# Another order of operations from the third batch on, in a linear-attention and leaky-ReLU MLP kernel on one Trainium2 core

## The chip, the cores and the metric

The kernel runs on one core of one Trainium2 chip. A core has five engines with a row of instructions each: TensorE (PE in the profile) for matrix products, VectorE (DVE), ScalarE (ACT), GpSimd (POOL), and SyncE (SP), which here only starts transfers (DMAs). The metric is the device time of one execution in microseconds (us). Before the change the median of 3 runs is 271.83 us, the lowest 271.36 and the highest 273.06.

## What is computed

A linear attention with cosine weights over 8 batch elements, 8 heads, 576 tokens and 64 channels, and a two-layer MLP (512 to 2048 to 512, leaky ReLU) on its result, 4608 tokens in all. All inputs and the output are 32-bit floats; the reference, cut to what matters:

```python
def phi(x, c, s):                       # c, s: cos and sin of pi/2 * position / 576
    r = np.maximum(x, 0.0)
    return np.concatenate([r * c, r * s], axis=-1)
q_p, k_p = phi(q, cos_w, sin_w), phi(k, cos_w, sin_w)
kv = np.einsum('bhsf,bhsd->bhfd', k_p, v)
z = np.sum(k_p, axis=2)
num = np.einsum('bhsf,bhfd->bhsd', q_p, kv)
den = np.einsum('bhsf,bhf->bhs', q_p, z)[..., None] + 1e-06
x = (num / den).transpose(0, 2, 1, 3).reshape(B * S, H * D)
h = x @ w_in
g = np.maximum(0.01 * h, h)
return g @ w_out
```

## The kernel before

**Groups of tokens.** The tokens are worked on in nine groups, g = 0 to 8. Groups 0 to 7 ("batch g") are the first 512 tokens of each batch element, in four parts j of 128; group 8 gathers the last 64 tokens of all eight elements. Each group goes through the same stages:

- q and k are loaded (`load(q,g)`, L280; `load(k,g)` and `load(v,g)`, L294). `q_prep(g,j,0,8,E)` (L418 on DVE or POOL, L416 on ACT) makes the two halves of phi(q), by the cosine and by the sine, for part j on engine E: D is DVE, A is ACT, P is POOL. `k_cos(b,j,E)` and `k_sin(b,j,E)` (the same lines) make one half of phi(k) each, for one of nine token columns j, and `v_pairs(b,lo,hi,E)` (L424 on ACT, L426 on the others) converts head pairs lo to hi of v to 16 bits, beside a column of ones that yields z.
- `kv_sum(b,0,4)` (L493) is phi(k)^T v: 72 small matmuls, two pairs of heads after the other two.
- phi(q) is transposed by DMA, two parts at a time: `q_transpose_dma(g,0)` for parts 0 and 1 and `q_transpose_dma(g,1)` for parts 2 and 3 (L530, qpT<-qp).
- `num(g,j)` (L577) multiplies the transposed phi(q) with kv, 8 matmuls; `den`, `rec` and `mul` (L587, L593, L601, all DVE) divide, which gives xs.
- `x_transpose_dma(g)` (L544, xT<-xs) transposes all four parts of x at once by DMA; batch 2 does it on PE with `x_transpose`.
- The first MLP layer is done by Strassen's scheme with seven products in place of eight, `P(g,u,n)` (L781): n is the product, 1 to 7, and u = 0 to 3 a quarter of the 2048 columns; each is 4 matmuls of 256 columns. `x_sum(g,n,E)` makes the sums of x that the scheme needs, and `w1_sum`, `weight_sum` those of the weights (all L674).
- `e(g,u,x)` brings the products out of PSUM, the memory that PE writes: b and s are copies (lower case on ACT, L424; capital on DVE, L426), w and y are additions on DVE (L674), and a, c, e and d are leaky ReLUs on ACT (L813) that write G.
- The second layer is done in the same way: `g_sum` makes sums of G (DVE), `F(g,i)` (L900) is half of a product, four matmuls, `R(g,n,E)` turns a finished product into a result (DVE additions L674; ACT copies L424), and `S(g,n)` (L964) stores a quarter of the group's output.

Groups 0 and 1 are done with other code (`M`, `h`, `f2` and others), which the change leaves alone, but F and R of batch 1 run beside batch 2 and 3 and are touched by the order.

**What sets the order.** Each operation is an entry in a long text, `PROGRAM` (L25 to L154), which is parsed and carried out entry by entry; the compiler may not reorder (`manual_schedule`). So every engine gets its instructions in the order of the entries, and works through them in that order: an instruction that waits holds up all behind it on its engine. Between engines there are only semaphores for the data and the buffers.

```python
    for name, args in parse(PROGRAM):
        OPS[name](*args)
```

All loads, stores and DMA transpositions of the part in question sit in one row on SyncE. The pools bound how far ahead it can be (the number is that of buffers):

```python
    stage = pool("stage", 4)
    kppool = pool("kpp", 1)
    qppool = pool("qpp", 2)
    qptpool = pool("qpT", 2)
    xspool = pool("xs", 1)
    xtpool = pool("xT", 2)
    opool = pool("osb", 4)
    ps_o = pool("ps_o", 2, PS)
    ps_n = pool("ps_n", 1, PS)
```

`stage` holds what the loads bring of q, k and v, and a load waits for the oldest of its four buffers. In PSUM, `ps_n` holds the two halves of one num or kv_sum, `ps_o` the sums of the second layer, and four more banks belong to P. These four open with batch 2's first product and use the memory that batch 1 had until then (`early`, closed in `banks`, L750), among it the sum that R(1,7) reads.

Of the kernel before, what the change touches and what calls it, by code (L numbers as in the profile page):

```python
# [55 lines left out]
g_sum(1,3,0,6) den(2,1) rec(2,1) k_sin(3,3,D) mul(2,1) R(1,6,D) k_cos(3,8,D) k_cos(3,5,P) k_sin(3,7,P) k_cos(3,0,P)
F(1,16) F(1,14) v_pairs(3,0,2,A) k_cos(3,3,A) q_prep(3,3,0,8,A) x_transpose(2,0,A) F(1,17) den(2,2) k_cos(3,2,D)
num(2,3) x_transpose(2,1,A) rec(2,2) mul(2,2) F(1,18) F(1,15) x_transpose(2,2,A) q_transpose_dma(3,0) load(q,4)
F(1,19) k_sin(3,2,D) k_cos(3,6,D) k_sin(3,6,A) k_cos(3,7,D) den(2,3) rec(2,3) v_pairs(3,2,4,D) mul(2,3) F(1,7)
# [1 line left out]
num(3,0) F(1,20) den(3,0) x_sum(2,2,P) rec(3,0) e(2,0,s) mul(3,0) P(2,0,6) P(2,0,2) F(1,21) P(2,1,1) x_sum(2,3,P)
q_transpose_dma(3,1) e(2,0,a) e(2,0,w) P(2,0,3) e(2,0,e) g_sum(1,4,0,8) num(3,1) x_sum(2,4,D) P(2,0,7) load(k,4)
P(2,1,5) F(1,22) e(2,1,b) den(3,1) rec(3,1) e(2,0,y) e(2,0,c) P(2,1,2) P(2,0,4) P(2,1,6) mul(3,1) e(2,1,S) e(2,1,a)
num(3,2) F(1,23) e(2,0,d) e(2,1,w) den(3,2) rec(3,2) mul(3,2) P(2,2,1) P(2,1,3) P(2,1,7) num(3,3) P(2,2,5) F(1,24)
R(1,4,D) den(3,3) q_prep(4,0,0,8,A) e(2,1,e) e(2,2,b) e(2,1,y) rec(3,3) P(2,2,6) mul(3,3) P(2,2,2) P(2,1,4) F(1,25)
e(2,2,s) e(2,1,c) e(2,1,d) e(2,2,w) e(2,2,a) P(2,2,3) w1_sum(1,3,D) P(2,3,1) q_prep(4,2,0,8,P) P(2,2,7) e(2,2,e)
P(2,3,5) load(v,4) q_prep(4,1,0,8,P) F(1,26) q_prep(4,3,0,8,D) e(2,2,y) g_sum(2,1,0,4,1) e(2,3,b) P(2,3,6) P(2,3,2)
F(1,27) e(2,3,s) k_cos(4,4,A) e(2,3,w) P(2,2,4) P(2,3,7) e(2,2,c) e(2,2,d) x_transpose_dma(3) P(2,3,3) F(2,0)
k_cos(4,7,D) g_sum(2,1,4,8,2) e(2,3,y) g_sum(2,2,4,8,2) e(2,3,a) x_sum(3,1,D) e(2,3,e) e(2,3,c) P(2,3,4) P(3,0,1)
k_cos(4,3,P) k_sin(4,3,P) x_sum(3,2,P) e(2,3,d) P(3,0,5) k_cos(4,1,A) k_sin(4,4,A) k_sin(4,1,A) e(3,0,s) R(1,3,D)  # L70
e(3,0,B) g_sum(2,1,5,8,2) g_sum(2,2,0,4,1) g_sum(2,2,5,8,2) F(2,1) P(3,1,1) F(2,2) P(3,0,6) P(3,0,2) F(2,3) F(2,4)
F(2,5) k_sin(4,8,A) k_cos(4,6,A) k_cos(4,8,A) e(3,0,a) R(2,1,A) e(3,0,w) x_sum(3,3,D) v_pairs(4,2,4,D) x_sum(3,4,D)
P(3,0,3) e(3,0,e) e(3,1,B) P(3,0,7) F(2,6) P(3,1,5) F(2,8) P(3,1,2) e(3,0,y) P(3,0,4) k_cos(4,0,A) k_sin(4,6,A)
k_sin(4,0,A) e(3,1,s) e(3,0,d) k_sin(4,2,P) k_cos(4,5,P) k_sin(4,5,D) v_pairs(4,0,2,D) F(2,7) P(3,1,6)
g_sum(2,3,0,4,1) e(3,1,w) R(2,6,D) e(3,0,c) e(3,1,a) k_cos(4,2,P) k_sin(4,7,P) load(q,5) q_transpose_dma(4,0)
# [5 lines left out]
P(3,2,7) x_transpose_dma(4) e(3,2,e) F(2,16) q_prep(5,0,0,8,P) q_prep(5,1,0,8,A) e(3,3,b) k_sin(5,1,D) R(2,7,D)
k_cos(5,4,D) e(3,2,y) e(3,3,s) q_transpose_dma(5,0) F(2,17) F(2,18) P(3,3,6) P(3,2,4) v_pairs(5,2,4,D) F(2,19)
load(k,6) e(3,3,w) e(3,2,c) q_prep(5,2,0,8,A) k_sin(5,8,A) g_sum(2,4,4,8) R(2,5,D) g_sum(2,4,0,4) k_sin(5,0,D) F(2,20)
P(3,3,7) F(2,21) P(3,3,2) e(3,2,d) q_prep(5,3,0,8,A) e(3,3,a) F(2,22) P(3,3,3) F(2,23) F(2,24) e(3,3,e) e(3,3,y)
F(2,25) P(4,0,1) k_sin(5,5,P) k_cos(5,7,P) e(4,0,b) x_sum(4,1,P) k_cos(5,0,P) F(2,26) P(3,3,4) P(4,0,5) F(2,27)
k_sin(5,3,D) v_pairs(5,0,2,D) R(2,4,D) q_transpose_dma(5,1) x_sum(4,3,D) x_sum(4,2,D) k_cos(5,2,A) e(3,3,c)
k_cos(5,3,D) R(2,3,D) e(3,3,d) e(4,0,s) F(3,0) P(4,0,6) P(4,0,2) F(3,1) e(4,0,w) g_sum(3,1,5,8,2) g_sum(3,1,0,4,1)
F(3,2) k_sin(5,4,A) k_cos(5,8,A) e(4,0,a) P(4,0,3) g_sum(3,3,5,8,2) g_sum(3,2,0,4,1) P(4,1,1) P(4,0,7) F(3,3) P(4,1,5)
q_prep(6,0,0,8,P) e(4,0,e) e(4,1,b) k_sin(5,2,A) x_sum(4,4,D) g_sum(3,2,5,8,2) R(3,1,A) e(4,0,y) g_sum(3,1,4,8,2)
g_sum(3,2,4,8,2) q_prep(6,1,0,8,A) e(4,1,S) F(3,4) kv_sum(5,0,4,n) e(4,0,c) P(4,1,6) P(4,1,2) F(3,5) P(4,0,4) e(4,1,w)  # L90
e(4,0,d) e(4,1,a) num(5,0) P(4,1,7) F(3,6) P(4,1,3) F(3,7) P(4,2,1) F(3,8) P(4,2,5) num(5,2) F(3,9) den(5,0) e(4,1,y)
P(4,1,4) rec(5,0) g_sum(3,3,4,8,2) k_cos(6,2,D) mul(5,0) g_sum(3,3,0,4,1) R(3,6,D) den(5,2) q_prep(6,2,0,8,A) e(4,1,c)
e(4,1,e) e(4,2,b) rec(5,2) P(4,2,6) F(3,10) mul(5,2) F(3,12) num(5,1) e(4,2,s) e(4,2,w) e(4,1,d) F(3,13) P(4,3,1)
F(3,11) P(4,2,2) P(4,2,3) num(5,3) F(3,14) den(5,1) k_cos(6,5,P) k_sin(6,6,A) k_cos(6,4,A) rec(5,1) g_sum(3,4,0,4)
mul(5,1) k_cos(6,0,D) k_sin(6,0,D) k_cos(6,7,P) k_sin(6,5,P) k_cos(6,3,P) den(5,3) k_sin(6,8,D) R(3,2,A) e(4,2,a)
k_cos(6,6,P) rec(5,3) k_cos(6,1,D) mul(5,3) F(3,16) P(4,3,5) P(4,2,7) e(4,2,e) S(2,4) load(v,6) S(2,5) S(2,3)
q_transpose_dma(6,0) S(2,2) x_transpose_dma(5) e(4,3,b) e(4,2,y) q_prep(6,3,0,8,A) e(4,3,S) load(q,7) P(4,3,6)
P(4,3,2) k_sin(6,1,P) k_sin(6,2,P) k_sin(6,4,D) e(4,3,w) F(3,17) F(3,15) P(4,2,4) F(3,18) S(3,2) P(4,3,3) k_sin(6,3,D)
F(3,19) e(4,3,a) k_cos(6,8,A) e(4,2,c) R(3,7,D) k_sin(6,7,D) g_sum(3,4,4,8) R(3,5,D) g_sum(4,1,4,8,2) F(3,20)
v_pairs(6,2,4,A) v_pairs(6,0,2,A) e(4,2,d) F(3,22) P(4,3,7) F(3,21) kv_sum(6,0,4,n) e(4,3,y) g_sum(4,1,0,4,1)  # L100
g_sum(4,2,0,4,1) x_sum(5,1,D) g_sum(4,2,4,8,2) x_sum(5,2,P) x_sum(5,3,P) F(3,23) P(4,3,4) R(3,4,D) e(4,3,c) e(4,3,e)
num(6,0) F(3,24) e(4,3,d) F(3,25) P(5,0,1) F(3,26) F(3,27) e(5,0,b) R(3,3,D) P(5,0,6) P(5,0,5) P(5,0,2) P(5,1,1)
F(4,0) e(5,0,S) g_sum(4,1,5,8,2) e(5,0,w) x_sum(5,4,D) den(6,0) rec(6,0) g_sum(4,2,5,8,2) e(5,0,a) F(4,1) F(4,2)
P(5,0,7) F(4,4) P(5,0,3) P(5,1,5) F(4,3) q_transpose_dma(6,1) F(4,5) num(6,1) e(5,0,e) R(4,1,A) mul(6,0) e(5,0,y)
e(5,1,B) den(6,1) q_prep(7,2,0,8,D) rec(6,1) mul(6,1) F(4,6) P(5,1,2) P(5,1,6) e(5,1,s) q_prep(7,0,0,8,A) F(4,8)
P(5,0,4) e(5,1,a) e(5,0,d) e(5,0,c) e(5,1,w) F(4,7) P(5,2,5) num(6,2) P(5,1,3) P(5,1,7) load(k,7) F(4,9)
g_sum(4,3,0,4,1) den(6,2) R(4,6,D) k_cos(7,8,D) rec(6,2) e(5,1,y) mul(6,2) e(5,2,S) e(5,1,e) F(4,10) F(4,11) P(5,2,1)
e(5,2,b) P(5,1,4) S(3,5) F(4,12) P(5,2,6) P(5,2,2) num(6,3) g_sum(4,3,5,8,2) R(4,2,A) e(5,1,d) e(5,2,a) e(5,1,c)
load(v,7) g_sum(4,3,4,8,2) e(5,2,w) q_prep(7,3,0,8,P) q_prep(7,1,0,8,P) F(4,13) k_sin(7,5,P) k_sin(7,1,P) k_cos(7,5,P)
den(6,3) k_sin(7,0,D) P(5,2,3) S(3,3) P(5,3,1) P(5,3,5) P(5,2,7) rec(6,3) mul(6,3) g_sum(4,4,0,4) e(5,2,e) e(5,2,y)  # L110
# [1094 lines left out]
```

## Time and profile before

| what | us |
|---|---|
| median of 3 runs | 271.83 |
| lowest, highest of them | 271.36, 273.06 |
| the profiled execution's own time | 273.01 |
| its span, first to last instruction | 271.2 |
| of the chain of work that ended last: PE, DMA | 86%, 9% |
| PE's granted clock, whole span | 1.00 |

The profile is that of one execution, which took 273.01 us in all; the times in its rows count from the start of its span of 271.2. The chain of work that ended last is found by going back from the last instruction to whatever released each one. Busy time is that of each engine, and a row of a group gives the line, the engine, the operation, the tile written and the tile read, the shape, and the number of instructions. The first 64 us or so of the span (groups 0 and 1, and kv_sum of batch 2) are the same in both kernels.

### The profile page before, as it was taken

To read this page: it belongs to the slowest core of one execution; us is meant where nothing else is said; L and a number is where in the kernel's file an instruction comes from. 1 tells how busy PE (TensorE), PEld (TensorE's weight loads), DVE (VectorE), ACT (ScalarE), POOL (GpSimd) and SP (SyncE) were. 2 spreads that over 40 slices of the span, in tenths; PEclk is the share of its full clock that TensorE was granted. 3 is DMA by queue.
4 is the path that set the end of the run, shared out by engine and by line. 5 is a ranking of instruction groups with operands and counts; after the bars stand their busy time and mean duration, and the time that the engine had idled before them with its cause. 6 is when DMAs were issued, how large, how long until landed. Compare 5 with 4: busy or idle time off the path is not lost.

```text
span 271.2 us, 7148 instructions
## 1 busy us (share of the span) xinstructions
PE 262.5 (97%) x2925; PEld 223.0 (82%) x2925; DVE 210.7 (78%) x446; ACT 174.0 (64%) x308; POOL 103.1 (38%) x87
## 2 busy tenths in 40 slices
...
GB/s 219 370 395 414 379 398 372 389 243 246 240 246 324 160 182 311 310 209 241 283 153 209 199 361 166 140 118 142 139 92 217 0 80 77 77 3 76 43 80 116
DMA packets 75040, 57.08 MB, mean 210 GB/s; under 512 B 47232, under 2 KB 63616, under 8 KB 74624
## 3 DMA queue, kind: packets, MB, share of 16 engines
...
q14 instruction: 9, 0.07, 0.1%
...
## 4 chain that ended last, share of the span: by engine, by line
PE 86%; DMA 9%; ACT 1%; DVE 1%; SPq 1%; issue 0%
PE ps L900 32%; PE ps_f L781 29%; PE ps_h L624 10%; PE ps_o L648 5%; DMA qpT<-qp 4%; DMA vst<-in_v_dram 3%; DMA xT<-xs 3%; PE ps_num L577 3%; PE ps_kv L493 2%; PE ps_f L900 1%; PE ps_xT L1054 1%; PE ps_kv L1005 1%; PE ps_numh L1040 1%; PE ps_qt L566 1%; PE ps_idle L358 0%; ACT vm L424 0%
## 5 line engine op out<-in xcount | busy, mean ns | idle before, releaser
L813 ACT ACTIVATE G<-ps_f 128x512 f16<-128x512 f32 x84 | 48.6, 597 | 31.0 <-PE ps_f L781 30.6
L900 PE MATMUL ps<-w,G 128*128 128x256 f16 x496 | 68.4, 273 | 0.0
L900 PEld LDWEIGHTS <-G 128*128 128x128 f16 x640 | 61.4, 98 | 6.2
L781 PEld LDWEIGHTS <-w 128*128 128x128 f16 x448 | 48.8, 114 | 2.2 <-DMA xT<-xs 0.7
L781 PE MATMUL ps_f<-xT,w 128*128 128x256 f16 x336 | 49.3, 273 | 1.0 <-DVE ext L674 0.5
L781 PEld LDWEIGHTS <-wsum 128*128 128x128 f16 x336 | 36.3, 114 | 0.7
L900 PE MATMUL ps<-T,ext 128*128 128x256 f16 x240 | 33.2, 273 | 0.0
L624 PE MATMUL ps_h<-xT,w 128*128 128x512 f16 (+1 forms) x144 | 29.1, 355 | 0.0
L900 PEld LDWEIGHTS <-ext 128*128 128x128 f16 x256 | 24.8, 98 | 2.6
L781 PE MATMUL ps_f<-X,wsum 128*128 128x256 f16 x176 | 26.2, 273 | 0.0
L674 DVE TENSOR_TENSOR ps_f<-ps_f,s 128x512 f32<-128x512 f32 x28 | 19.5, 695 | 8.1 <-PE ps_f L781 5.8
L624 PEld LDWEIGHTS <-w 128*128 128x128 f16 x144 | 15.9, 114 | 10.9
L418 POOL TENSOR_SCALAR kp<-kst,cos_t 128x256 f16<-128x256 f32 (+1 forms) x17 | 20.8, 1229 | 7.7 <-PE ps_f L781 3.0
L674 DVE TENSOR_TENSOR y<-ps_f,s 128x512 f32<-128x512 f32 x28 | 19.1, 682 | 5.0 <-PE ps_f L781 4.9
L418 POOL TENSOR_SCALAR kp<-kst,sin_t 128x256 f16<-128x256 f32 x15 | 18.5, 1239 | 5.9 <-DMA kst<-in_k_dram 5.9
L635 ACT ACTIVATE G<-ps_h 128x1024 f16<-128x1024 f32 x16 | 15.9, 1022 | 7.2 <-PE ps_h L624 7.2
L674 DVE TENSOR_TENSOR osb<-ps,ext 128x512 f32<-128x512 f32 x23 | 15.7, 685 | 5.0 <-PE ps L900 4.9
L601 DVE TENSOR_TENSOR xs<-ps_num,rden 128x512 f16<-128x512 f32 x28 | 19.2, 687 | 0.5
L813 ACT ACTIVATE G<-y 128x512 f16<-128x512 f32 x28 | 17.7, 631 | 3.0 <-DVE y L674 2.9
L424 ACT COPY ps_f<-ps_f 128x512 f32<-128x512 f32 x22 | 12.5, 570 | 8.6 <-PE ps_f L781 7.7
L900 PE MATMUL ps<-ext,G 128*128 128x256 f16 x128 | 17.7, 273 | 0.0
L424 ACT COPY s<-ps_f 128x512 f32<-128x512 f32 x21 | 12.4, 589 | 7.5 <-DVE y L674 4.1
(120 smaller groups left out, 451.3 us busy)
## 6 DMA issues: line engine op xcount, KB each, us to landing
...
qst<-in_q_dram SPq DMA_DIRECT2D x7, 1024.0 KB, 10.3
kst<-in_k_dram SPq DMA_DIRECT2D x5, 1152.0 KB, 7.3
vst<-in_v_dram SPq DMA_DIRECT2D x5, 1152.0 KB, 9.1
w2st<-in_moe_w_out_dram SPq DMA_DIRECT2D x3, 1024.0 KB, 13.9
...
```

What stands on the lines that cost most here:

```text
L418: eng.tensor_scalar(out=o, in0=i, scalar1=0.0, scalar2=col, op0=ALU.max, op1=ALU.mult)
L424: nc.scalar.copy(o, i)
L493: nc.tensor.matmul(ps[:, o, (c - lo) * NE : (c - lo + 1) * NE], lhsT=st["kp", b][sl, c, j, :], rhs=vm[sl, c, j, :], start=(j == 0), stop=( ...
L577: nc.tensor.matmul(ps[lo:hi, h // 4, (h % 4) * NE : (h % 4 + 1) * NE], lhsT=qpT[:, h, lo:hi], rhs=kv[b][:, h, :],)
L601: nc.vector.tensor_tensor(out=xs(), in0=ps[:, :, 0 : 4 * NE].rearrange("p a (b e) -> p a b e", e=NE)[:, :, :, 0:D], in1=st["rden", *k].rea ...
L624: nc.tensor.matmul(ps[:, m % 2, lo:hi], lhsT=w1[m // 4, c][0][:, w1[m // 4, c][1], m % 4 : 512 : 4], rhs=xT[:, lo // P : hi // P, c, :], s ...
L635: nc.scalar.activation(st["g", g][:, m - 1 : m + 1, :], ps, AF.Lrelu)
L648: nc.tensor.matmul(st["ps_o", g, tt], lhsT=st["g", g][:, m, tt * P : (tt + 1) * P], rhs=w2[:, m, :], start=(m == 0), stop=(m == NFT - 1),)
L674: eng.tensor_tensor(out=o, in0=a, in1=b, op=op)
L781: nc.tensor.matmul(ps[:, mi * HT : (mi + 1) * HT], lhsT=a[:, c, 2 * r0 + mi : 512 : 4], rhs=b[:, c], start=(n in (1, 5) and mi == 0 and c ...
L813: nc.scalar.activation(st["g", g][:, m : m + 2, r * HT : (r + 1) * HT], {"a": A, "c": y22, "e": E, "d": B_}[e].rearrange("p (m t) -> p m t ...
L900: nc.tensor.matmul(ps[:, tt], lhsT=a[:, i, tt * P : (tt + 1) * P], rhs=b[:, i], start=(first and i == 4 * halves[0]), stop=(i == NPR - 1 a ...
```

## The change

The entries of `PROGRAM` behind `num(2,0)` (L52) stand in another order, up to the end; the functions stay as they are. The entries are the same 1128, and PE's row has the same 5852 instructions, weight loads with them, in another order. 66 entries get another engine: 17 go from DVE to ACT, 12 from POOL to ACT, 11 from POOL to DVE, 10 from DVE to POOL, 8 from ACT to DVE and 8 from ACT to POOL. By kind they are 22 k_cos, 20 k_sin, 10 copies of e (6 from DVE to ACT, 4 back), 8 x_sum, 3 v_pairs and 3 q_prep. Three places of the diff, with the rest left out:

```diff
...
-k_cos(3,4,D) x_transpose(2,3,A) kv_sum(3,0,4,n) R(1,2,D) x_sum(2,1,D) R(1,7,D) R(1,5,D) P(2,0,1) e(2,0,b) P(2,0,5)
...
+x_transpose(2,3,A) kv_sum(3,0,4,n) R(1,7,D) x_sum(2,1,D) R(1,2,D) R(1,5,D) x_sum(2,2,D) P(2,0,1) e(2,0,b) load(q,4)
...
-load(k,5) S(1,4) S(1,5) q_transpose_dma(4,1) load(v,5) S(1,2) S(1,3) load(q,6) kv_sum(4,0,4,n) P(3,1,3) P(3,1,7)
...
+v_pairs(4,2,4,A) P(3,0,4) P(3,1,2) e(3,0,d) load(k,5) q_transpose_dma(4,0) load(q,5) e(3,1,w) F(2,7) R(2,6,D)
...
+k_cos(5,0,A) q_prep(5,1,0,8,A) k_cos(5,5,A) q_prep(5,2,0,8,A) e(3,2,c) x_transpose_dma(4) load(q,6) F(2,17) P(3,3,6)
...
```

**DVE at the start of batch 2's products.** The rows run from the last conversions for kv_sum(3) to the results of batch 1. vm<-vst is v_pairs(3,2,4); the first osb row is R(1,2), ext<-ps_7 is R(1,7), the second osb row R(1,5), and X1<-xT is x_sum(2,1). Before:

```order
L426 CAST vm_167<-vst_1079 128x18x64
L601 TENSOR_TENSOR xs_1194<-ps_num_1236,rden_1280 128x512
L418 TENSOR_SCALAR kp_1117<-G0_95,cos_t_159 128x4x64
L674 TENSOR_TENSOR osb_1368<-ps_7_1081,ext_93 128x512
L674 TENSOR_TENSOR X1_179<-xT_1227 128x512
L674 TENSOR_TENSOR ext_93<-ps_7_1111,ext_93 128x512
L674 TENSOR_TENSOR osb_1372<-ps_7_1167,ext_93 128x512
```

Now:

```order
L593 RECIPROCAL rden_1278<-den_1270 128x8
L601 TENSOR_TENSOR xs_1176<-ps_num_1233,rden_1278 128x512
L674 TENSOR_TENSOR ext_93<-ps_7_1111,ext_93 128x512
L674 TENSOR_TENSOR X1_179<-xT_1220 128x512
L674 TENSOR_TENSOR osb_1368<-ps_7_1081,ext_93 128x512
L674 TENSOR_TENSOR osb_1370<-ps_7_1168,ext_93 128x512
L674 TENSOR_TENSOR X2_180<-xT_1220,X1_179 128x512
```

R(1,7) has moved from behind R(1,2) and x_sum(2,1) to ahead of them, right behind mul(2,3) (xs); a half of k and v_pairs(3,2,4) have left the place, and a second x_sum has come to it.

**SyncE from the transposition of batch 3's x to that of batch 4's.** qst, kst and vst are the loads of q, k and v, first of batch 5 and, in the last qst row, of q of batch 6; out_0_dram rows are stores of batch 1. Before, where qp_1539 is the first pair of q's parts of batch 4 and qp_1578 the second:

```order
L544 DMA_TRANSPOSE xT_1629<-xs_1411 128x16x128
L280 DMA qst_1771<-in_q_dram 128x8x256
L530 DMA_TRANSPOSE qpT_1773<-qp_1539 128x16x128
L294 DMA kst_1775<-in_k_dram 128x4x576
L964 DMA out_0_dram<-osb_1535 128x2x256
L964 DMA out_0_dram<-osb_1372 128x2x256
L530 DMA_TRANSPOSE qpT_1779<-qp_1578 128x16x128
L294 DMA vst_1781<-in_v_dram 128x4x576
L964 DMA out_0_dram<-osb_1368 128x2x256
L964 DMA out_0_dram<-osb_1668 128x2x256
L280 DMA qst_1785<-in_q_dram 128x8x256
L544 DMA_TRANSPOSE xT_2008<-xs_1898 128x16x128
```

Now, where qp_1586 is the second pair:

```order
L544 DMA_TRANSPOSE xT_1626<-xs_1411 128x16x128
L530 DMA_TRANSPOSE qpT_1727<-qp_1586 128x16x128
L294 DMA kst_1765<-in_k_dram 128x4x576
L530 DMA_TRANSPOSE qpT_1767<-qp_1539 128x16x128
L280 DMA qst_1769<-in_q_dram 128x8x256
L964 DMA out_0_dram<-osb_1535 128x2x256
L964 DMA out_0_dram<-osb_1368 128x2x256
L294 DMA vst_1913<-in_v_dram 128x4x576
L964 DMA out_0_dram<-osb_1370 128x2x256
L964 DMA out_0_dram<-osb_1641 128x2x256
L544 DMA_TRANSPOSE xT_2023<-xs_1879 128x16x128
L280 DMA qst_2025<-in_q_dram 128x8x256
```

The second pair of q of batch 4 has moved ahead of the first, right behind batch 3's x; the load of k,5 now stands between the two, and that of q,5 behind both. Batch 4's x, which was behind the load of q,6, now stands ahead of it. Behind these rows the next transposition of q (batch 5) and the load of k,6 follow in both.

**DVE at the first half of batch 6's k.** kp<-kst is k_cos(6,2); ps_f2<-ps_f3,s5 is the addition e(4,1,w), whose result is read on the way to product P(4,1,7); den and rden belong to num(5,0). Before:

```order
L426 COPY s5_183<-ps_f2_1380 128x512
L674 TENSOR_TENSOR ps_f2_1380<-ps_f3_1381,s5_183 128x512
L587 TENSOR_SCALAR den_2358<-ps_num_2308 128x8
L674 TENSOR_TENSOR y22_184<-ps_f3_1381,s5_183 128x512
L593 RECIPROCAL rden_2365<-den_2358 128x8
L674 TENSOR_TENSOR G1_96<-G1_96 128x2x256
L418 TENSOR_SCALAR kp_2368<-kst_2050,cos_t_159 128x4x64
```

Now:

```order
L418 TENSOR_SCALAR qp_2193<-qst_2025,cos_t_159 128x8x64
L418 TENSOR_SCALAR qp_2193<-qst_2025,sin_t_160 128x8x64
L674 TENSOR_TENSOR G1_96<-G1_96 128x2x256
L418 TENSOR_SCALAR kp_2303<-kst_2129,cos_t_159 128x4x64
L674 TENSOR_TENSOR ext_93<-ext_93,G1_96 128x2x256
L674 TENSOR_TENSOR ps_f2_1379<-ps_f3_1380,s5_183 128x512
```

k_cos(6,2) has moved from five rows behind e(4,1,w) to two rows ahead of it; the copy ahead of e(4,1,w), e(4,1,S), has gone to ACT, and q_prep(6,0), the two qp rows, has come from POOL.

More of the change, by code (lines that the diff above doesn't have):

```diff
@@ L56 @@
[L56 to L59, printed above, removed]
-k_cos(3,4,D) x_transpose(2,3,A) kv_sum(3,0,4,n) R(1,2,D) x_sum(2,1,D) R(1,7,D) R(1,5,D) P(2,0,1) e(2,0,b) P(2,0,5)
@@ L61 @@
[L61 to L75, printed above, removed]
@@ L81 @@
[L81 to L95, printed above, removed]
@@ L96 @@
[L96 to L110, printed above, removed]
@@ new lines @@
+F(1,1) F(1,9) F(1,5) F(1,10) num(2,1) F(1,3) q_prep(3,0,0,8,A) q_prep(3,1,0,8,A) k_sin(3,3,A) R(1,1,A) F(1,11) F(1,6)
+F(1,12) k_cos(3,1,D) rec(2,0) mul(2,0) k_sin(3,8,P) load(v,3,2,4) store_held() F(1,13) num(2,2) g_sum(1,3,0,6)
+den(2,1) rec(2,1) k_cos(3,6,D) k_cos(3,8,D) mul(2,1) R(1,6,D) k_cos(3,0,P) F(1,14) k_sin(3,1,A) q_prep(3,3,0,8,A)
+v_pairs(3,0,2,A) x_transpose(2,0,A) F(1,16) F(1,17) den(2,2) k_cos(3,3,A) num(2,3) x_transpose(2,1,A) rec(2,2)
+mul(2,2) k_sin(3,4,P) F(1,18) F(1,15) x_transpose(2,2,A) q_transpose_dma(3,0) k_sin(3,2,P) k_sin(3,6,A) k_sin(3,7,D)
@@ new lines @@
+k_cos(4,6,D) g_sum(2,3,5,8,2) x_sum(3,4,P) F(2,8) P(3,1,5) P(3,1,6) k_cos(4,3,A) k_sin(4,0,A) k_sin(4,2,P) e(3,1,s)
+v_pairs(4,2,4,A) P(3,0,4) P(3,1,2) e(3,0,d) load(k,5) q_transpose_dma(4,0) load(q,5) e(3,1,w) F(2,7) R(2,6,D)
+g_sum(2,3,0,4,1) kv_sum(4,0,4,n) P(3,1,7) e(3,1,a) P(3,1,3) num(4,0) P(3,2,1) den(4,0) rec(4,0) e(3,1,e) mul(4,0)
+F(2,12) P(3,2,5) F(2,9) num(4,1) e(3,0,c) e(3,1,y) g_sum(2,3,4,8,2) den(4,1) rec(4,1) e(3,2,S) S(1,4) mul(4,1) S(1,2)
+load(v,5) S(1,5) S(1,3) e(3,2,b) P(3,2,2) F(2,13) F(2,10) P(3,1,4) q_prep(5,0,0,8,A) e(3,2,a) P(3,2,6) e(3,2,w)
```

141 lines of the change are left out of this document (90 added, 51 removed).

## The prediction

> **What bounds the kernel now.** I read the page's head first (which engine is busy), then the busy time by stretches (where TensorE is not), then the timeline and the waits around those places. Clock times are us from the start of the profiled span.
>
> ```profile
> PE 262.5 (97%) x2925; PEld 223.0 (82%) x2925; DVE 210.7 (78%) x446; ACT 174.0 (64%) x308; POOL 103.1 (38%) x87
> ```
>
> TensorE (PE) is busy for 97% of the span. The change touches only what comes after the third batch's first num, soon after 64, so the next table is cut from there. Its columns are the stretch and its length, then the busy us of PE, weight loads, VectorE (DVE), ScalarE (ACT) and GpSimd (POOL), then PE's granted clock and the DMA engines' share.
>
> ```profile
> 64.00:76.00 12.00, 12.00 (x199) 10.81 (x199) 11.37 (x31) 10.40 (x17) 6.50 (x5) 1.00 0.92 254
> 76.00:100.00 24.00, 23.51 (x300) 22.43 (x299) 22.23 (x44) 19.29 (x38) 18.04 (x11) 1.00 0.95 231
> 100.00:125.00 25.00, 23.82 (x299) 21.99 (x298) 19.89 (x43) 19.31 (x38) 15.19 (x13) 1.00 1.11 259
> 125.00:250.00 125.00, 125.00 (x1439) 117.08 (x1438) 99.12 (x208) 78.05 (x141) 40.94 (x29) 1.00 0.58 144
> 250.00:271.20 21.20, 17.15 (x158) 15.35 (x155) 10.23 (x19) 3.75 (x7) 0.00 (x0) 1.00 0.30 90
> ```
>
> In the changed part PE is idle for 24.00 - 23.51 = 0.49 and 25.00 - 23.82 = 1.18, and then for 125 us not at all, at the full clock. The 4.05 in the last stretch are the last result's addition and store. The timeline of PE shows the three idle places; in brackets stands what ended each:
>
> ```profile
> 76.22 1.32 PE L493 MATMUL ps_kv<-vm,kp 64*128 64x66 f16 x72
> 78.03 0.63 PE L781 MATMUL ps_f<-xT,w 128*128 128x256 f16 x4 [0.49 <-DVE ext L674]
> 109.47 0.60 PE L900 MATMUL ps<-w,G 128*128 128x256 f16 x4
> 110.77 0.43 PE L577 MATMUL ps_num<-kv,qpT 128*128 128x66 f16 x8 [0.71 <-DMA qpT<-qp]
> 120.46 1.04 PE L900 MATMUL ps<-w,G 128*128 128x256 f16 x8
> 121.97 0.63 PE L781 MATMUL ps_f<-xT,w 128*128 128x256 f16 x4 [0.47 <-DMA xT<-xs]
> ```
>
> Busy time hides part of such a wait, because matmuls overlap. Two rows of the chain of work that ended last give the pace without waits:
>
> ```profile
> 180.25 1.25 PE ps_kv L493 x72
> 254.49 7.42 PE ps L900 x68
> ```
>
> A matmul of 256 columns starts every 7.42 / 68 = 0.109, and a kv_sum takes 1.25. By starts, then, the waits cost 78.03 - (76.22 + 1.25) = 0.56, 110.77 - (109.47 + 4 x 0.109) = 0.86 and 121.97 - (120.46 + 8 x 0.109) = 0.64. Together 2.06: the most that another order can win here, since the number and the shapes of PE's instructions stay.
>
> **The change, part by part.**
>
> *The first wait (78.03).* P(2,0,1), the first product of batch 2, takes over PSUM that R(1,7) still has to read. DVE before it:
>
> ```profile
> 76.10 0.69 DVE L674 TENSOR_TENSOR osb<-ps,ext 128x512 f32<-128x512 f32 x1 [0.28 <-PE ps L900]
> ...
> 77.28 0.68 DVE L674 TENSOR_TENSOR ext<-ps,ext 128x512 f32<-128x512 f32 x1
> ```
>
> R(1,2) (first row) and an x_sum stand ahead of R(1,7) (second), which ends at 77.96. The new order puts R(1,7) first: it starts near 76.1 and ends near 76.8, before kv_sum ends at 77.47. Three conversions also leave DVE there; one of them, v_pairs(3,2,4), goes to POOL, which was busy for only 6.50 of the 12.00 up to 76:
>
> ```profile
> L426 POOL CAST w<-ext 128x1024 f16<-128x1024 f32 x4 | 4.7, 1189 | 0.7 <-DMA ext<-in_moe_w_in_dram 0.6
> ```
>
> At 1189 ns for 1024 columns its 1152 take about 1.34 (an estimate), which fits. Gain 0.56; what is late next is kv_sum's own end.
>
> *The second wait (110.77).* num(4,3) waits for the transposition of q's second half of batch 4, which I call qT(4,1). SyncE's queue around it, then the landings of all qT, of all xT, and of two kinds of loads:
>
> ```profile
> 88.81 1.74 SPq L544 DMA_TRANSPOSE xT<-xs  x1
> ...
> 91.96 5.46 SPq L530 DMA_TRANSPOSE qpT<-qp  x1
> 97.55 0.50 SPq L294 DMA_DIRECT2D kst<-in_k_dram  x1
> ...
> 101.09 5.47 SPq L530 DMA_TRANSPOSE qpT<-qp  x1
> ...
> 109.23 0.71 SPq L280 DMA_DIRECT2D qst<-in_q_dram  x1
> 114.45 4.84 SPq L544 DMA_TRANSPOSE xT<-xs  x1
> ```
> ```profile
> DMA to landing us min/median/max: 4.3/4.7/9.8
> ```
> ```profile
> DMA to landing us min/median/max: 4.3/4.4/7.5
> ```
> ```profile
> qst<-in_q_dram SPq DMA_DIRECT2D x7, 1024.0 KB, 10.3
> kst<-in_k_dram SPq DMA_DIRECT2D x5, 1152.0 KB, 7.3
> ```
>
> The medians of both transpositions are near their minimum; the long ones are those with a load of 1 MB just ahead, as here (qT(4,1): 110.77 - 101.09 = 9.7; the batch's xT: 121.97 - 114.45 = 7.5). Now the pair is turned: qT(4,1) goes first, right after xT of batch 3, with no load ahead. It waits for q_prep(4,3) on DVE:
>
> ```profile
> 89.90 0.66 DVE L418 TENSOR_SCALAR qp<-qst,cos_t 128x512 f16<-128x512 f32 x1
> 90.47 0.69 DVE L418 TENSOR_SCALAR qp<-qst,sin_t 128x512 f16<-128x512 f32 x1
> ```
> ```profile
> 90.26 1.29 POOL L418 TENSOR_SCALAR kp<-kst,cos_t 128x256 f16<-128x256 f32 x1
> ```
> ```profile
> 105.90 0.42 PE L577 MATMUL ps_num<-kv,qpT 128*128 128x66 f16 x8
> ```
>
> q_prep(4,3) now stands behind a g_sum and a y addition of some 0.7 each, so it ends near 92.6 instead of 91.16. qT(4,1) is then issued until 94.4 (1.74, like the xT at 88.81), load(k,5) until 94.9, and qT(4,0) stands behind that load. At 9.8 after its issue, the slowest of all, it lands at 104.7; num(4,0) needs it at 105.90. So the old wait of 0.86 goes, and the new one costs nothing if that holds. The other end is the old qT(4,1), which landed 110.77 - 97.55 = 13.2 after the load ahead of it, with two stores in between: 94.4 + 13.2 = 107.6, a wait of 1.7. No store stands between now, so I take 0.2.
>
> *The third wait (121.97).* xT of batch 4 is late because load(q,6), issued at 109.23, was ahead of it. Now load(q,6) comes behind it, and xT lands about 4.4 after its issue, at 118.9. P(4,0,1) would start at 121.33. Gain 0.64, with 2.4 to spare. What pays is load(q,6), some 7 later, and on the queue behind it qT(5,0), load(k,6) and qT(5,1). The first reader of q,6 stands some ten us after that issue, which the 10.3 of such loads just fits: cost nothing, at worst a DVE wait like rival B's.
>
> *The 66 moved operations.* 17 go from DVE to ACT, 12 from POOL to ACT, 11 from POOL to DVE, 10 from DVE to POOL, 8 each from ACT to DVE and to POOL. Most are halves of k (instruction, then least, median and longest ns):
>
> ```profile
> L418 POOL TENSOR_SCALAR kp<-kst,cos_t x17: 713/1142/1663, 11.7 to 167.5; 128x256 f16<-128x256 f32 x16, 128x128 f16<-128x128 f32 x1
> L418 DVE TENSOR_SCALAR kp<-kst,cos_t x15: 302/343/569, 52.0 to 176.4; 128x256 f16<-128x256 f32 x15
> L416 ACT ACTIVATE kp<-kst,sin_t x14: 496/508/540, 62.4 to 178.2; 128x256 f16<-128x256 f32 x14
> ```
>
> ACT takes 29 and gives 16, at about 0.5 each: 6.5 us more on an engine that was busy for 78 of 125 while PE never stopped. This cover is gone where an operation is the last before a kv_sum. The tightest such place is kv_sum(4), whose second half now needs v_pairs(4,2,4) from ACT, late in ACT's row:
>
> ```profile
> L424 ACT CAST vm<-vst 128x1152 f16<-128x1152 f32 x5 | 5.6, 1149 | 0.0
> ```
>
> Between 0 and the half of it that kv_sum's own first half (0.62) doesn't cover, about 0.5; I take 0.2. For all other places together I take 0.2 too, between nothing and two such waits, as PE's 125 us without a pause are the nearest row.
>
> *The end.* Behind the last F the order is as before, so the 4.05 stay.
>
> Sum: -0.56 - 0.86 - 0.64 + 0.2 + 0.2 + 0.2 = -1.46. The profiled execution took 273.01 for its span of 271.2, so it would take 271.55. It stands 1.18 above the median of the runs, 271.83; for the median the forecast is 271.83 - 1.46 = 270.4.
>
> *A rule against it.* q_prep(4,3) ran beside POOL: its second row began 0.21 into POOL's 1.29 and ended 0.39 before POOL did, so it did not wait for POOL's instruction to end. The Trainium skill, "SBUF — State Buffer", section "Who interferes with whom", says that a two-port DVE instruction and a GpSimd one exclude each other for the whole instruction, which would be rival D's time. The trace contradicts it at this place.
>
> **The rivals.**
>
> *A: the wait moves to num(4,0).* qT(4,0) is now second of its pair. Landing as in the slow row above costs 1.7 instead of 0.2: 271.83 - 1.46 + 1.5 = 271.9. For it speaks that only 1.2 us are to spare at best, against it that no store stands between. It begins when qT(4,0) lands after 105.9.
>
> *B: load(k,6) comes too late, slower than before.* On DVE k_cos(6,2), which came three us after e(4,1,w), now stands two rows ahead of it. This is e(4,1,w) before:
>
> ```profile
> 131.10 0.70 DVE L674 TENSOR_TENSOR ps_f<-ps_f,s 128x512 f32<-128x512 f32 x1
> ```
>
> Load(k,6) now stands behind load(q,6) and a crowded qT(5,0): 114.45 + 1.74 + 0.71 + 5.47 = 122.4, landing at 129.7 (7.3) or, as slowly as the q loads, 132.7 (10.3). DVE comes to k_cos(6,2) near 130.2 and blocks until then. PE's product P(4,1,7) behind e(4,1,w) stands four products (1.75) later than before, so up to some 132 this is free. With a load 13.2 long, like the pair above, it lands at 135.6 and PE waits 3.6: 270.4 + 3.6 = 274.0. Against it: no load of the page's groups has such a median.
>
> *C: the timed runs have less to win.* The profiled run may have waits that the median run has not (273.01 against 271.83). With half of 2.06 there, the forecast is 271.83 - 1.03 + 0.6 = 271.4.
>
> *D: DVE waits for whole POOL instructions.* If each half of q_prep(4,3) waits for a k half of 1.29 on POOL, it ends 2.6 later, and qT(4,0) lands at 107.3, 1.4 too late: 270.4 - 0.2 + 1.4 = 271.6. The rows above speak against it.
>
> **How the numbers follow.** My forecast 0.55 at 270.4 (own range 269.2 to 271.2), A 0.17 at 271.9, B 0.10 at 274.0, C 0.10 at 271.4, D 0.03 at 271.6; a gain beyond all three waits 0.02, something unseen that costs over 2 us 0.03. The low end is 271.83 - 2.06, less the 0.47 by which the fastest run lies under the median: 269.3, taken as 269.2. The high end, 272.7, takes in A, C and D and a part of B's smaller waits. About 1% is what a measurement of this kernel can tell from no change: faster by that (under 269.1) 0.04, slower (over 274.5, half of B's upper part and the unseen) 0.07, within it 0.89.
>
> **What would show it.** In the new profile no wait of PE names "ext" or "xT", and "qpT" at most 0.2; xT of batch 4 lands within 5; PE is idle for under 0.5 between 76 and 125. Wrong: PE waiting for over 1 us at the first ps_num of batch 4 (A, D), DVE waiting for "kst" near 130 and PE behind it (B), or an idle PE anywhere from 125 to 250.

## The result, and the profile after

The changed kernel takes 270.86 us in the median of 20 runs, the kernel before 272.62 in the median of 20. The ratio is 0.9947, with a 95% interval of 0.993 to 0.9964: 1.4 us less, between 1.0 and 1.9. (The medians differ by 1.8, the means of the runs by 1.4.) A gain of half a per cent is the size that was forecast (1.46 us). The profiled execution of the changed kernel took 270.42 for a span of 268.6.

The head of its page, to be held against that of before:

```profile
PE 262.4 (98%) x2925; PEld 223.2 (83%) x2925; DVE 207.6 (77%) x439; ACT 179.2 (67%) x321; POOL 93.5 (35%) x81
```

PE has the same busy time, ACT has 5 us more and POOL 10 us less, DVE 3 us less. Busy time by stretches, columns as before:

```profile
64.00:76.00 12.00, 11.94 (x198) 10.76 (x192) 10.13 (x28) 11.09 (x20) 7.42 (x6) 1.00 1.00 254
76.00:100.00 24.00, 24.00 (x303) 22.99 (x300) 21.41 (x43) 20.09 (x39) 18.12 (x12) 1.00 0.92 233
100.00:125.00 25.00, 25.00 (x313) 23.37 (x311) 22.62 (x49) 22.23 (x44) 7.41 (x6) 1.00 0.99 252
125.00:250.00 125.00, 125.00 (x1439) 117.18 (x1438) 95.69 (x200) 79.08 (x144) 38.27 (x26) 1.00 0.62 144
250.00:268.60 18.60, 14.84 (x136) 13.16 (x134) 9.16 (x17) 3.26 (x6) 0.00 (x0) 0.99 0.34 100
```

The 0.49 and 1.18 us in which PE was idle between 76 and 125 are gone; from 64 to PE's end its only idle time is now 0.06, ahead of 76. PE's timeline at the three spots, and the kv_sum of batch 2, which ends just ahead of the change and serves below as the zero of time:

```profile
63.65 1.32 PE L493 MATMUL ps_kv<-vm,kp 64*128 64x66 f16 x72
...
75.88 1.32 PE L493 MATMUL ps_kv<-vm,kp 64*128 64x66 f16 x72
77.13 0.63 PE L781 MATMUL ps_f<-xT,w 128*128 128x256 f16 x4
...
109.52 0.42 PE L577 MATMUL ps_num<-kv,qpT 128*128 128x66 f16 x8
...
119.68 0.60 PE L781 MATMUL ps_f<-xT,w 128*128 128x256 f16 x4
```

The rows are kv_sum(2), kv_sum(3), P(2,0,1), num(4,3) and P(4,0,1). P(2,0,1) starts 1.25 behind kv_sum(3), the kv_sum's own length; num(4,3) and P(4,0,1) have no wait in brackets. What stood ahead of each, on DVE (R(1,7), then the two halves of q_prep(4,3)) and on SyncE's queue:

```profile
75.76 0.69 DVE L674 TENSOR_TENSOR ext<-ps,ext 128x512 f32<-128x512 f32 x1 [0.89 <-PE ps L900]
...
90.82 0.60 DVE L418 TENSOR_SCALAR qp<-qst,cos_t 128x512 f16<-128x512 f32 x1
91.34 0.48 DVE L418 TENSOR_SCALAR qp<-qst,sin_t 128x512 f16<-128x512 f32 x1
```
```profile
91.96 1.96 SPq L530 DMA_TRANSPOSE qpT<-qp  x1
94.01 1.24 SPq L294 DMA_DIRECT2D kst<-in_k_dram  x1
95.45 5.96 SPq L530 DMA_TRANSPOSE qpT<-qp  x1
...
113.22 2.49 SPq L544 DMA_TRANSPOSE xT<-xs  x1
115.81 0.52 SPq L280 DMA_DIRECT2D qst<-in_q_dram  x1
116.44 5.66 SPq L530 DMA_TRANSPOSE qpT<-qp  x1
122.19 0.54 SPq L294 DMA_DIRECT2D kst<-in_k_dram  x1
```

R(1,7) ends at 76.45, ahead of the kv_sum's end. For the second qT row, qT(4,0), and for the xT the view of that one tile says:

```profile
DMA to landing us min/median/max: 7.9/7.9/7.9
```
```profile
DMA to landing us min/median/max: 4.5/4.5/4.5
```

qT(4,0) lands at 95.45 + 7.9 = 103.35, 1.7 ahead of num(4,0) at 105.07. xT lands at 117.7, 2.0 ahead of P(4,0,1).

From the first kv_sum row to PE's end the profiled executions differ by 203.07 - 201.19 = 1.88 us (before: 250 + 17.15 - 64.08; now: 250 + 14.84 - 63.65). The whole spans differ by 2.6; of that 0.43 lies ahead of the first changed entry, and 0.29 behind PE's last matmul, where the order is the same. These 0.72 are no work of the change.

### The profile page after: what moved, and what is told of

It reads as the page before. It is cut to its first block, busy times and chain, and to the rows that moved or that the text cites. A ratio compares the mean times of both kernels' runs of the same rounds, so it can differ in the third digit from the quotient of the medians.

```text
span 268.6 us, 7148 instructions
## 1 busy us (share of the span) xinstructions
PE 262.4 (98%) x2925; PEld 223.2 (83%) x2925; DVE 207.6 (77%) x439; ACT 179.2 (67%) x321; POOL 93.5 (35%) x81
## 4 chain that ended last, share of the span: by engine, by line
PE 90%; ACT 4%; DMA 3%; DVE 1%; SPq 1%; issue 0%; ACTq 0%
PE ps L900 33%; PE ps_f L781 32%; PE ps_h L624 10%; PE ps_o L648 5%; PE ps_kv L493 3%; DMA vst<-in_v_dram 3%; PE ps_num L577 2%; ACT qp L416 2%; PE ps_f L900 1%; ACT vm L424 1%; PE ps_xT L1054 1%; PE ps_kv L1005 1%; PE ps_numh L1040 1%; PE ps_qt L566 1%; PE ps_idle L358 0%; SPq L280 0%
## 5 line engine op out<-in xcount | busy, mean ns | idle before, releaser
L900 PE MATMUL ps<-T,ext 128*128 128x256 f16 x240 | 34.0, 273 | 0.0
L418 POOL TENSOR_SCALAR kp<-kst,sin_t 128x256 f16<-128x256 f32 x16 | 20.6, 1296 | 11.6 <-PE ps_kv L493 6.2
L418 POOL TENSOR_SCALAR qp<-qst,cos_t 128x512 f16<-128x512 f32 (+1 forms) x6 | 11.5, 1911 | 23.1 <-DMA qpT<-qp 18.8
L674 POOL TENSOR_TENSOR X<-xT,X 128x512 f16<-128x512 f16 x6 | 7.7, 1281 | 27.7 <-PE ps_f L781 23.8
## 6 DMA issues: line engine op xcount, KB each, us to landing
ext<-in_moe_w_in_dram SPq DMA_DIRECT2D x4, 512.0 KB, 10.7
```

Source lines behind the costliest of these rows:

```text
L418: eng.tensor_scalar(out=o, in0=i, scalar1=0.0, scalar2=col, op0=ALU.max, op1=ALU.mult)
L674: eng.tensor_tensor(out=o, in0=a, in1=b, op=op)
L900: nc.tensor.matmul(ps[:, tt], lhsT=a[:, i, tt * P : (tt + 1) * P], rhs=b[:, i], start=(first and i == 4 * halves[0]), stop=(i == NPR - 1 a ...
```

## The experiments

The theory at this point is the prediction's: three waits of PE, each removed by its own part of the order, which add up. Twelve runs followed: ten other kernels, and the two kernels themselves once more (e7, e8). The ratio is against the kernel before; `D`, `A`, `P` in a diff are DVE, ACT and POOL.

**e1: R(1,7) first, alone.**

```diff
-kv_sum(3,0,4,n) R(1,2,D) x_sum(2,1,D) R(1,7,D) R(1,5,D) P(2,0,1)
+kv_sum(3,0,4,n) R(1,7,D) R(1,2,D) x_sum(2,1,D) R(1,5,D) P(2,0,1)
```

> The kernel before with one entry moved: R(1,7) right behind kv_sum(3), ahead of R(1,2). Three-waits theory (the change gains by the three waits of PE in the first profile, each by itself): the wait of 0.5 us of ps_f on DVE's ext is gone, the other two stay, and the time is 0.5 to 0.6 us less than before (ratio near 0.998). Rival, the moved engines: without k_cos(3,4) and v_pairs(3,2,4) leaving DVE, R(1,7) still ends behind kv_sum, and 0.2 us or more of the wait stay.

Measured: 0.9998 (0.9979 to 1.0017), no gain that can be seen, though the interval reaches to a gain of 0.57, so that the times alone would not exclude the 0.56. The wait on ext is gone, with every conversion still on its old engine, so the rival falls. PE's timeline, kv_sum(2) and all the waits behind it:

```profile
63.90 1.32 PE L493 MATMUL ps_kv<-vm,kp 64*128 64x66 f16 x72
...
110.63 0.43 PE L577 MATMUL ps_num<-kv,qpT 128*128 128x66 f16 x8 [1.24 <-DMA qpT<-qp]
121.56 0.63 PE L781 MATMUL ps_f<-xT,w 128*128 128x256 f16 x4 [0.20 <-DMA xT<-xs]
```

PE came to num(4,3) earlier and waited there 1.24 in place of 0.71: num(4,3) itself starts 46.73 behind kv_sum(2), and 46.69 in the kernel before. P(4,0,1) starts 121.56 - 63.90 = 57.66 behind kv_sum(2); before it was 121.97 - 64.08 = 57.89. Of 0.56 us only 0.2 arrived. This is where the theory of three waits that add up began to fall. The new one: **P(4,0,1) starts when batch 4's x lands, and what is won ahead of that is waited away.**

**e8: the kernel before once more, for a second profile.**

> The kernel before as it is, for a second profile. Three-waits theory: the same three waits, 0.56, 0.86 and 0.64 us, each within 0.3. Rival C of the prediction: the two that hang on DMA landings differ from run to run, and at least one is under half of what the first profile showed, so that the median run has less to win than 2.06.

Measured: one run of 272.65. Its timeline:

```profile
63.82 1.32 PE L493 MATMUL ps_kv<-vm,kp 64*128 64x66 f16 x72
...
77.78 0.63 PE L781 MATMUL ps_f<-xT,w 128*128 128x256 f16 x4 [0.49 <-DVE ext L674]
121.68 0.63 PE L781 MATMUL ps_f<-xT,w 128*128 128x256 f16 x4 [1.08 <-DMA xT<-xs]
```

The wait at num(4,3) is not in this list, and that at xT is twice as long as in the first profile: rival C's single waits do differ. But P(4,0,1) starts at 121.68 - 63.82 = 57.86, within 0.03 of the first profile. The single waits differ from run to run, their end does not.

**e2: x's transposition ahead of load(q,6), alone.**

```diff
-load(v,5) S(1,2) S(1,3) load(q,6) kv_sum(4,0,4,n)
...
-P(3,2,7) x_transpose_dma(4) e(3,2,e)
+load(v,5) S(1,2) S(1,3) kv_sum(4,0,4,n)
...
+P(3,2,7) x_transpose_dma(4) load(q,6) e(3,2,e)
```

> The kernel before with one entry moved: load(q,6) right behind the transposition of batch 4's x on SyncE's queue. Three-waits theory: batch 4's xT lands within 5 us of its issue in place of 7.5, the wait of 0.5 to 0.6 us of ps_f on xT is gone, the time is about 0.6 us less (ratio near 0.998). Rival, a wait that moves: load(q,6), some 6 us later, pushes q's transposition for batch 5 and the load of k,6, and PE waits behind DVE or num(5,0) by as much; the time is the same.

Measured: 0.9986 (0.9969 to 1.0004). xT landed 5.0 behind its issue, PE did not wait for it, and P(4,0,1) started 56.58 behind kv_sum(2) in the profile, 1.3 earlier than before. That is more than the 0.64 of the wait itself, since the wait at num(4,3) was short in this profile, as in that of e8. The interval of the times, however, reaches from no gain to 0.8 us. In a run whose qT(4,1) lands as late as in e1, about half would be lost again at num(4,3); that is argued from e1's rows, no profile of e2 shows it. The rival, a wait that moves, does not show in this profile; it does in e9 below.

**e3: the pair of batch 4's q turned, alone.**

```diff
-load(q,5) q_transpose_dma(4,0) load(k,5) S(1,4) S(1,5) q_transpose_dma(4,1) load(v,5) S(1,2) S(1,3) load(q,6)
+q_transpose_dma(4,1) load(k,5) q_transpose_dma(4,0) load(q,5) S(1,4) S(1,5) load(v,5) S(1,2) S(1,3) load(q,6)
```

> The kernel before with the order on SyncE's queue as in the changed kernel for batch 4's q: qT(4,1), load(k,5), qT(4,0), load(q,5) in place of load(q,5), qT(4,0), load(k,5), qT(4,1). Three-waits theory: the wait of 0.86 us at num(4,3) is gone, num(4,0) does not wait, the time is about 0.9 us less (ratio near 0.997). Rival A of the prediction: qT(4,0), second of its pair, is late and num(4,0) waits for 1 us or more; the time is not less than before.

Measured: 0.9962 (0.9943 to 0.9982), 1.0 us less. Num(4,3) does not wait, nor num(4,0). PE does not wait for xT either, though load(q,6) is still ahead of it: the queue runs earlier. The issues of the pair took 5.46 and 5.47, each behind a load; now the first, with no load ahead, takes 2.08 and the second 6.11. SyncE's rows for load(q,6) and xT:

```profile
105.29 0.99 SPq L280 DMA_DIRECT2D qst<-in_q_dram  x1
113.46 3.75 SPq L544 DMA_TRANSPOSE xT<-xs  x1
```

Load(q,6) is issued at 105.29 - 63.94 = 41.35 behind kv_sum(2), where it was 45.15; with landings 12.1 and 5.8 behind the issue it lands at 53.45 and xT at 55.32. The only wait left is that of 0.56 on ext, and P(4,0,1) starts at 56.41. Rival A falls.

**e4 and e9: all three edits, and all but the first.**

> All three edits together on the kernel before, nothing else. Three-waits theory: no wait of PE from 64 us on is longer than 0.2, the ratio is that of the whole change, 0.993 to 0.996. Rival, the rest of the order and the 66 engines: they matter by themselves, and the three edits give less than half of the gain (ratio above 0.997), with other waits in the profile.

> The kernel before with two of the three edits: the pair of batch 4's q turned and load(q,6) behind batch 4's x; R(1,7) stays behind R(1,2). Theory that one landing sets the time (P(4,0,1) starts when batch 4's xT lands, whatever was won ahead of it): with that landing early, the wait of 0.56 us on R(1,7) counts in full, so the way from kv_sum(2) to kv_sum(5) is 63.5 us, 0.5 to 0.6 longer than with all three edits, and about as with the pair alone; ratio 0.996 to 0.998. Rival: R(1,7) is worth nothing in either case; 62.9 us, ratio as with all three.

Measured: e4 0.9957 (0.9942 to 0.9973), e9 0.9972 (0.995 to 0.9995). In the profiles P(4,0,1) starts 55.86 behind kv_sum(2) with all three and 56.41 without R(1,7) first; from kv_sum(2) to kv_sum(5) it is 62.94 and 63.50. So R(1,7), which brought 0.2 alone, is worth its 0.55 once xT lands early; this rests on one profile of each, as the two intervals of the times overlap. And the three edits alone, without the other moved entries and the 66 engines, have the whole change's ratio within their interval.

The profile of e9 shows a price of putting x ahead of load(q,6). PE's waits from 64 us on:

```profile
PE ps_f L781 <- DVE ext L674: 0.5, 1, 0.5
PE ps_f L781 <- ACT ps_f L424: 0.3, 1, 0.3
```

The second is new. The later load holds up qT(5,1) behind it, which lands 68.44 behind kv_sum(2), where it is 65.91 in e3. ACT's q_prep(6,2) waits for the buffer that qT(5,1) reads (0.62, to 132.05), and the copy e(4,2,b) behind it comes late for product P(4,2,6). In e4 the same product starts 0.29 behind the pace of the products ahead of it, though the view of waits has no row for it. From kv_sum(5) to PE's end it is 138.52 in e9 and 138.36 in e4, against 138.07 in e3 and in the kernel before. This is e2's rival, a wait that moves, in a size of 0.3 to 0.45.

**e10: the changed kernel with load(q,6) ahead of x again.**

```diff
-x_transpose_dma(4) load(q,6) F(2,17)
+load(q,6) x_transpose_dma(4) F(2,17)
```

> The changed kernel with one entry moved back: load(q,6) ahead of the transposition of batch 4's x on SyncE's queue. Theory that one landing sets the time: the load is issued some 6 us earlier and x's transposition, at the same time as before, lands 1 to 2 us later than in the changed kernel, near 55.3 to 56 from the start of kv_sum(2); PE comes to P(4,0,1) near 55.5, so the wait is 0 to 0.6 us and the ratio 0.995 to 0.997. Rival, the load alone makes the transposition late: xT lands as late as before, at 57.6 or later, PE waits for 2 us, and the time is that of before.

Measured: 0.9942 (0.9922 to 0.9963), as the changed kernel. xT is late, as forecast, but not late enough:

```profile
64.06 1.32 PE L493 MATMUL ps_kv<-vm,kp 64*128 64x66 f16 x72
...
120.09 0.60 PE L781 MATMUL ps_f<-xT,w 128*128 128x256 f16 x4
```
```profile
113.62 4.17 SPq L544 DMA_TRANSPOSE xT<-xs  x1
```
```profile
DMA to landing us min/median/max: 6.2/6.2/6.2
```

It lands at 113.62 + 6.2 - 64.06 = 55.76, and P(4,0,1) starts at 56.03, the same as in the changed kernel, with 0.27 to spare. Putting x ahead of load(q,6) brings nothing here by itself; the turned pair of q has already done it.

The profiles of these kernels side by side, in us behind the start of kv_sum(2) (landing is issue plus time to landing; the last matmul is PE's end):

| kernel | load(q,6) lands | xT(4) lands | P(4,0,1) starts | last matmul ends | ratio |
|---|---|---|---|---|---|
| before | 55.45 | 57.87 | 57.89 | 203.07 | |
| e8, before again | 55.39 | 57.83 | 57.86 | 203.04 | |
| e1, R(1,7) first | 55.17 | 57.61 | 57.66 | 202.84 | 0.9998 |
| e2, x ahead of q,6 | 58.48 | 54.69 | 56.58 | 201.83 | 0.9986 |
| e3, pair turned | 53.45 | 55.32 | 56.41 | 201.57 | 0.9962 |
| e9, e2 and e3 | 58.70 | 53.92 | 56.41 | 202.02 | 0.9972 |
| e4, all three | 57.99 | 53.17 | 55.86 | 201.30 | 0.9957 |
| e10, after, q,6 ahead | 53.95 | 55.76 | 56.03 | 201.18 | 0.9942 |
| after | 58.66 | 54.07 | 56.03 | 201.19 | 0.9947 |
| e7, after again | 58.84 | 53.95 | 56.21 | 201.38 | 0.9948 |

Wherever load(q,6) is ahead of it on the queue, xT lands 1.8 to 2.4 behind that load, whenever it was issued; where the load comes behind it, xT takes 4.2 to 5.0 from its own issue. In the first three rows P(4,0,1) follows the landing by 0.02 to 0.05; in the others the landing is at least 0.27 ahead of it, and P(4,0,1) has to wait for its turn on PE alone. The second profiles of the two kernels tell how far a profile repeats: to 0.03 and 0.19 at PE's end. The times show less than the profiles (e2 0.4 against 1.2, all three 1.2 against 1.8); what the other executions pay is not shown. The Trainium skill, "DMA: Bandwidth & Descriptors", section "Queues, rings and completion order", says that a DMA's completion signal is written only after every earlier write of the same DMA engine. These rows agree: the transposition is never signalled ahead of the load in front of it.

**e7: the changed kernel once more.**

> The changed kernel as it is, for a second profile and times on the same chip as the two runs ahead. All theories: ratio 0.993 to 0.9965; PE without a wait over 0.2 us from 64 us on. If the transposition qT(4,0) lands later than in the first profile by over 1.7 us, num(4,0) waits, which would tell what the slower of the changed kernel's runs pay.

Measured: 0.9948 (0.9933 to 0.9963). The view of PE's waits from 64 on has no row, and qT(4,0) lands 1.8 ahead of its reader.

**e5 and e6: the engines without the order, and the order without the engines.** The 66 entries change only their last letter, for instance `e(3,3,s)` to `e(3,3,S)`.

> The order of before with the 66 engines of the changed kernel. Three-waits theory: the waits on qpT and xT stay as they are, the wait on ext is shorter by what leaves DVE ahead of R(1,7) (0 to 0.5 us), and the time is the same or up to 0.5 us less (ratio 0.998 to 1.000). Rival, the engines carry the gain: ratio under 0.997. Second rival: operations that are late on ACT in an order that was not made for them cost PE new waits, ratio over 1.001.

> The order of the changed kernel with the engines of before. Three-waits theory: none of the three waits comes back in full, since each went by an order; up to 0.3 us at R(1,7), as v_pairs(3,2,4) and a half of k are on DVE again; ratio 0.994 to 0.997. Rival, the engines carry it: PE waits again ahead of kv_sum(4) or P(2,0,1) for over 0.5 us, ratio over 0.998.

Measured: 1.0195 (1.0174 to 1.0216) and 1.0451 (1.0417 to 1.0484): 5.3 us and 12.3 us slower. Neither rival named such a size. In e5 the second rival holds: new waits, two of the longest behind ACT. Of the old three only that on ext is left in its profile, with the 0.5 of before, so the moved engines alone do not free R(1,7). In e6 the ratio is on the rival's side, but not its places: PE waits neither ahead of kv_sum(4) nor at P(2,0,1); its longest waits are of 2.7 and 2.3, on DVE's ps_f and ext. PE waits in e5, among others, for a half of k that stands too late in ACT's row for kv_sum(4):

```profile
74.06 0.43 PE L577 MATMUL ps_num<-kv,qpT 128*128 128x66 f16 x8 [1.01 <-DVE xs L601]
...
98.53 0.28 PE L900 MATMUL ps<-w,G 128*128 128x256 f16 x1 [0.84 <-ACT G L813]
107.80 1.26 PE L493 MATMUL ps_kv<-vm,kp 64*128 64x66 f16 x68 [1.53 <-ACT kp L416]
```

**e11 and e12: which engines the order needs.** The changed kernel, with the 48 halves of k, q and v on their old engines (e11), and with the 18 copies of e and x_sums on theirs (e12).

> The changed kernel with the 48 moved halves of k, q and v on their old engines; the copies of e and x_sum as changed. If the cost of the new order on the old engines (12.3 us) lies in the kv_sums and what feeds them: 8 us slower or more than before, PE waiting at kv_sum and behind copies that stand behind a late half on ACT or DVE. If it lies in the evacuation of the products: 3 us or less.

> The changed kernel with the 18 moved copies of e and x_sum on their old engines; k, q and v as changed. The other half of the same question: 3 us slower than before or less if the halves of k carry the cost, 8 or more if the copies and sums do. In both, if the two parts add, the costs of this and the run ahead, each against the changed kernel's time, sum to 13.7 us.

Measured: 1.0199 (1.0158 to 1.024) and 1.0393 (1.0354 to 1.0432), so 6.9 and 12.2 us more than the changed kernel. Against the kernel before, e12 is 10.7 slower, which is the case in which the copies and sums carry the cost. E11 is 5.4 slower, between its two cases, so the halves of k, q and v cost as well. The two do not add: they sum to 19 where e6, which takes both back, costs 13.7. The two longest waits of e12, of 3.52 and 2.44, stand in e6 too, with 2.7 and 2.3; that waits of the two kinds cover each other would fit, but is not shown, since the profile of e11 tells nothing of its waits (last section). In e12 the longest is on PE:

```profile
124.97 1.01 PE L781 MATMUL ps_f<-xT,wsum 128*128 128x256 f16 x4 [3.52 <-DVE ps_f L674]
```

DVE there waited for the copy e(3,3,s), which is back on ACT, behind q_prep(5,3):

```profile
122.39 0.71 ACT L416 ACTIVATE qp<-qst,cos_t 128x512 f16<-128x512 f32 x1
123.01 0.71 ACT L416 ACTIVATE qp<-qst,sin_t 128x512 f16<-128x512 f32 x1
123.62 0.57 ACT L424 COPY s<-ps_f 128x512 f32<-128x512 f32 x1
```

In the changed kernel that copy is on DVE, and q_prep(5,3) may stand where it does. This wait cost more than its length, by the clock behind it (last section). The second longest is on a product of the second layer:

```profile
235.70 1.47 PE L900 MATMUL ps<-ext,G 128*128 128x256 f16 x12 [2.44 <-DVE ext L674]
```

It goes back to x_sum(8,2), which is on DVE again and waits there for x_sum(8,1) on POOL, and so for the transposition of group 8's x; the result of F behind it on DVE waits with it. In the changed kernel it stands on POOL, where nothing is behind it but sums of the same x:

```profile
234.62 0.43 DVE L674 TENSOR_TENSOR X<-xT,X 128x512 f16<-128x512 f16 x1 [3.25 <-POOL X L674]
234.96 0.68 DVE L674 TENSOR_TENSOR ext<-ps,ext 128x512 f32<-128x512 f32 x1
```

## Why the prediction was right, and where its sum was not

- **Total.** Forecast 1.46 less, measured 1.0 to 1.9 less; 270.4 against 270.86, within the range. Since the three runs shown beforehand had a median of 271.83 and twenty have 272.62, the time came out a little above the forecast while the gain came out on it. Part of that is luck: the sum had 2.06 for the waits and 0.6 for new ones, of which none was seen in the changed kernel. The profiled executions differ by 1.88 on PE, and the interval of the gain holds that as well as 1.46, so the times do not tell the two apart.
- **The three waits as a sum.** This step was wrong. All three are removed, and 2.06 is rightly the most that is to be won, but "gain 0.56", "0.86" and "0.64" are not what the three edits bring. The three waits sit one behind the other ahead of a single date, the landing of batch 4's x. Alone, the edits moved P(4,0,1) by 0.2, 1.5 and 1.3 us in the profiles, in the order of the waits, together by 2.0 and not by 3.0. The times alone (0.05, 1.0 and 0.4; together 1.2, each known to some 0.5) could still be a sum, so this rests on the profiles.
- **The first wait.** Mechanism right (R(1,7) ends ahead of kv_sum, POOL takes v_pairs in time), its worth conditional: 0.2 alone (e1), 0.55 behind the others (e9 against e4).
- **The second wait.** Right in direction and in the reading of the queue, too small in size: turning the pair also pulls load(q,6) forward by 2.0 and xT by 2.5 us (e3), so that it carries most of the change alone: 1.0 of 1.4 in the times, 1.5 of 1.9 to PE's end. The 0.2 for num(4,0) was not needed. q_prep(4,3) ended at 91.82, ahead of the 92.6 that was worked out, and qT(4,0) landed in 7.9, not 9.8.
- **The third wait.** xT landed 4.5 behind its issue (4.4 forecast), with 2.0 to spare (2.4 forecast). But with the pair turned this part is worth nothing (e10), and on the old order it has a price of 0.3 to 0.45 on ACT (e9, e4), where the prediction put the later load at nothing. In the changed kernel no such wait is seen.
- **The 66 engines.** The 0.2 each for kv_sum(4) and for all other places measured nothing: no wait of PE over 0.2 from 76 us on. That holds for order and engines together only: the prediction priced the moved operations by their mean durations, and on the old order the same engines cost 5.3 us (e5).
- **The rivals.** A fell: num(4,0) had 1.7 to spare. B fell as to PE, and DVE did what it said, for 1.58 us:

```profile
128.96 0.35 DVE L418 TENSOR_SCALAR kp<-kst,cos_t 128x256 f16<-128x256 f32 x1 [1.58 <-PE ps_f L781]
129.22 0.42 DVE L674 TENSOR_TENSOR ext<-ext,G 128x512 f16<-128x512 f16 x1
129.56 0.69 DVE L674 TENSOR_TENSOR ps_f<-ps_f,s 128x512 f32<-128x512 f32 x1
```

  This is k_cos(6,2), and e(4,1,w) two rows behind it. The row names PE as the releaser, but load(k,6), issued at 122.19, lands 6.6 later at 128.8, just ahead of the start, so the load fits as the cause better; the row does not show it. Load(k,6) was forecast for 129.7 to 132.7, and DVE for 130.2; both came sooner, and up to some 132 the block was to be free on PE. It was. C: e8 shows that single waits do differ between runs, but not their end (57.86 against 57.89), so half of 2.06 was not missing. D fell: q_prep(4,3)'s halves took 0.60 and 0.48 while POOL was in the halves of k, and waited for none of them. Such a half takes 0.48 with POOL idle (at 195.68 in the kernel before), so beside POOL it took 0.12 longer here, and 0.2 longer at the place that the prediction shows:

```profile
89.11 4.08 POOL L418 TENSOR_SCALAR kp<-kst,sin_t 128x256 f16<-128x256 f32 x3
```
